# Output weights' scale through GpSimd ahead of the scores, two conversions moved into slots, and 40 idle products on PE before block 0's value product

## The chip, the cores and the metric

One core of a Trainium2 chip runs the kernel. The metric is device time in microseconds (us) of one launch. A profiled execution gives, beside its own time, a trace of each engine: PE (TensorE, matrix products; PEld is its weight load), DVE (VectorE), ACT (ScalarE), POOL (GpSimd) and SP (SyncE, which here only issues DMAs).

## What is computed

An attention layer and two feed-forward layers, in float32, on 12,288 tokens of width 128:

```python
kv_pool = kv.reshape(B, H // 4, 4, W // 4, 4, C).mean(axis=(2, 4))   # 768 keys
k = v = kv_pool.reshape(B, -1, C) @ w_sr
a = softmax(q @ k.T / sqrt(C));  x = a @ v
h = x @ moe_w_in;   g = h * clip(h + 3, 0, 6) / 6;   x = g @ moe_w_out    # 128 -> 2048 -> 128
h = x @ moe2_w_in;  g = where(h >= 1, h, where(h <= -1, 0, (h + 1)**2 / 4))
out = g @ moe2_w_out
```

## The kernel before

**Split numbers.** Each factor of the large products is cut into a high and a low part (fp16 in attention's value product and layer 0, fp32r elsewhere) and three products are summed. Weights are cut on the chip. For layer 0 they are scaled first by a power of two and a unit taken from the largest magnitude of the whole matrix; this needs a maximum over all 128 partitions. `mw[1]` collects it for layer 0's output weights, `w_sc[1]` holds the scales (`ws` in the rows).

**Weight conversion.** A piece is 128 x 512 numbers, 16 pieces j0 to j15: of layer 0 the pieces j0, j2, j4, j6 are input weights, j1, j3, j5, j7 output weights. A conversion has four stages: j.0 two ACT passes (L237, L241 or L244), j.1 two DVE passes (L251, L253) and a GpSimd add (L255), j.2 one DVE pass (L261), j.3 the high part on ACT (L272) and the low part on GpSimd (L275; for j5 on DVE).

**Order.** `tc.manual_schedule()` keeps on each engine the order in which the code records instructions, so an engine that waits holds everything behind it. Waits between engines come from the tiles: whoever reads or writes a tile waits for its earlier writer or readers, and a tile counts as a whole. The work has two phases.

*Prologue* (about 0 to 64 us): the string `PROLOGUE` names steps one by one: pooling of kv, keys, block 0's scores (s, S), maxima (n, N), exponentials (e), the normalised weights' high and low part (a, b; b also issues the DMA transpose into `at`), the scale of v (vm, vr, vs), its high part on ACT (vh, L405) and low part on DVE (vl, L410) out of the PSUM tiles `vps` (`acc` in the rows), the value product (x0, x1, L533) and the first conversions. Steps m1, m3, m5, m7 are the four DVE maxima over the output weights (L178), oa their row maximum (L184). ot and ob find the maximum over the partitions with a PE transpose, a DVE reduction and a PE product with `ones` (L193, L197, L198), oc makes the scales (L205 to L214), hs the layer's factors `h_sc` and `o_sc`. For the input weights the same maximum goes through GpSimd (ia: L184, L187).

*Slots.* Slot T handles a 256-wide piece of layer 0's hidden width, and from T = 11 also one of layer 1: `m_in` (L554) on PE, `relu1` on ACT (L597), `mul1` on DVE (L603), the split `hi_lo` on ACT and GpSimd (L631, L633), `m_out` (L570) on PE; a block of 512 tokens takes 8 slots. A slot also carries steps of the next blocks' scores (L461, L472, L497), normalisation (L505 to L518) and value product. `conv_step` starts a conversion in each slot listed in `CONV_AT` and moves each one in flight on by a stage.

Of the kernel before, what the change touches and what calls it, by code (L numbers as in the profile page):

```python
# [8 lines left out]
FP32 = mybir.dt.float32  # L9
# [6 lines left out]
ALU = mybir.AluOpType  # L16
AX = mybir.AxisListType
# [8 lines left out]
KV_MODE = "DDVVPPPPPPPP"  # L26
PROLOGUE = """
m0 k0 k1 m2 m4 m6 ia k2 ib g2 k4 k3 j0.0 g3 t1 j2.0 j0.1 k5 p1 q0 k6 z1 t2 j0.2 j2.1 p2 t0 j0.3 k7 p0
z0 j2.2 j4.0 k8 t3 z2 j2.3 k9 j4.1 p3 s0 y3 k10 z3 j4.2 j6.0 y2 k11 n0 t4 j4.3 y1 s2 t5 j6.1 p4
p5 n2 z4 z5 y5 s1 j6.2 y4 n1 y0 S2 S0 N0 m1 S1 N1 j6.3 s3 n3 N2 e0 e1 vm S3 a0 vr b0 e2 a1 m3  # L30
N3 e3 a2 b1 vs a3 vh b2 b3 vl m5 m7 oa ot q1 ob oc hs j1.0 x0 j1.1 j3.0 x1 j1.2 j3.1 j1.3 j3.2 j5.0 j3.3
j5.1
"""
N_ST = 6
W_DT = (FP16, F32R)

H_SC = 2.0 ** -22
# [13 lines left out]
def tile_attn_moe_moe2(  # L51
# [15 lines left out]
    nc = tc.nc  # L67
# [20 lines left out]
    sm_p = ctx.enter_context(tc.tile_pool(name="sm", bufs=3))  # L88
# [29 lines left out]
    def new_h():  # L118
        return ps_h.tile([128, 512], FP32, tag="h", name="h")
# [50 lines left out]


    mw = [const.tile([128, 4], FP32, name=f"mw{n}") for n in range(4)]
    w_tops = {}

    def w_max(job):
        m, which, i = job
# [2 lines left out]
                                axis=AX.X, op=ALU.max, apply_absolute_value=True)  # L179

    def w_top(n):
        nc.vector.tensor_reduce(out=mw[n][:, 0:1], in_=mw[n], axis=AX.X, op=ALU.max)  # L184

    def w_top_pool(n):
        nc.gpsimd.partition_all_reduce(mw[n][:, 1:2], mw[n][:, 0:1], channels=128,  # L187
                                       reduce_op=bass_isa.ReduceOp.max)
        w_tops[n] = mw[n][:, 1:2]

    def w_top_row(n):
        w_tops[n] = new_h()
        nc.tensor.transpose(w_tops[n][0:1, 0:128], mw[n][:, 0:1], ident)  # L193

    def w_top_all(n):
        m1 = sm_p.tile([1, 1], FP32, tag="wtop", name="wtop")
        nc.vector.tensor_reduce(out=m1, in_=w_tops[n][0:1, 0:128], axis=AX.X, op=ALU.max)  # L197
        nc.tensor.matmul(w_tops[n][:, 128:129], ones, m1)  # L198
        w_tops[n] = w_tops[n][:, 128:129]

    def w_scales(n):
        sc, u, v = w_sc[n], w_sc[n].bitcast(U32), mw[n].bitcast(U32)
        nc.vector.tensor_scalar(out=mw[n][:, 0:1], in0=w_tops[n], scalar1=2.0 ** -14, scalar2=None,  # L205
                                op0=ALU.max)
# [524 lines left out]
    with tc.manual_schedule():  # L731
        nc.scalar.dma_start(out=wsr, in_=w_sr)
        load_next()
        make_identity(nc, ident)
        nc.vector.memset(ones, 1.0)
        nc.vector.tensor_reduce(
            out=pool_m.rearrange("p (a q) -> p a q", a=4),
            in_=ident.rearrange("p (a r q) -> p a q r", a=4, r=4), axis=AX.X, op=ALU.add,
        )
        nc.vector.tensor_scalar(out=pool_m, in0=pool_m, scalar1=1.0 / 16.0, scalar2=None, op0=ALU.mult)  # L740
        mem = {}

# [76 lines left out]
```

## Time and profile before

| | |
|---|---|
| three timed runs | 1333.38, 1334.45, 1334.20 us, median 1334.2 |
| profiled execution | 1333.9 us, of it 1332.1 us span (first to last instruction) |
| busy in the span | PE 1279.0, DVE 1145.1, ACT 1049.2, POOL 1017.3 us |
| granted PE clock, mean | 0.987 of 2.4 GHz |

The page's busy times are means over unlike stages. A stretch of the trace is read by itself: which engine is busy in it throughout, and, where none is, which instruction ends each wait.

### The profile page before, as it was taken

The page shows a single profiled execution, that of the slowest core. Times are in us where ns is not written, and L with a number is a line of the kernel's source. Part 1 is how long each engine was busy: PE and PEld are TensorE (multiplying, and loading weights), DVE is VectorE, ACT ScalarE, POOL GpSimd, SP SyncE. Part 2 cuts the span into 40 slices and gives each one's busy share as a digit, 9 for nine tenths or more (in the row PEclk, how much of TensorE's full clock was granted, in tenths as well). Part 3 has the DMA queues.
Part 4 walks back from the last instruction along what each step waited for, and adds up shares of the span by engine and source line. Part 5 has one row for each costly group of instructions (what it writes and reads, how often), then busy time and mean ns, then how long its engine had stood idle before and what let it go on. Part 6 is the DMA issues. An engine that isn't in the chain of part 4 may idle for free.

```text
span 1332.1 us, 18501 instructions
## 1 busy us (share of the span) xinstructions
PE 1279.0 (96%) x6250; PEld 843.8 (63%) x6250; DVE 1145.1 (86%) x1851; ACT 1049.2 (79%) x1917; POOL 1017.3 (76%) x826
## 2 busy tenths in 40 slices
PE   6578899999999999999999999999999999999998
PEld 5434566666666666666666666666666666666666
DVE  4789998898888888989989889888888899898677
ACT  2588988887788788788878778887887888788776
POOL 1278897787787787877878877877877778787886
PEclk9789999999999999999999999999999999999999
DMA  9633122222221212212123122222312121121001
GB/s 327 149 78 66 28 43 45 40 44 44 41 44 32 52 33 44 48 29 51 36 40 52 33 44 40 45 39 45 42 35 52 32 45 36 32 45 24 8 9 16
DMA packets 260783, 66.28 MB, mean 50 GB/s; under 512 B 252368, under 2 KB 256592, under 8 KB 260688
## 3 DMA queue, kind: packets, MB, share of 16 engines
q1 hardware_dynamic: 257888, 63.73, 24.9%
q10 hardware_dynamic: 2800, 1.38, 0.4%
q8 instruction: 49, 0.80, 0.3%
q14 instruction: 46, 0.38, 0.1%
HBM read 21.04 MB, written 6.29 MB: 21 GB/s over the span
## 4 chain that ended last, share of the span: by engine, by line
PE 82%; DVE 5%; ACT 2%; issue 1%; POOL 0%; POOLq 0%; ACTq 0%; DVEq 0%
PE acc L570 35%; PE h L554 35%; PE s L461 6%; PE s L533 6%; DVE g L610 1%; DVE g L620 1%; DVE t L603 1%; ACT t L597 1%; ACT h L631 1%; DVE a L518 1%; POOL l L633 0%; DVE wa L251 0%; DVE nm L472 0%; ACT g L616 0%; DVE wst L261 0%
## 5 line engine op out<-in xcount | busy, mean ns | idle before, releaser
L633 POOL TENSOR_TENSOR l<-g,h 128x512 fp32r<-128x512 f32 x382 | 503.0, 1337 | 238.8 <-ACT h L631 111.7
L633 POOL TENSOR_TENSOR l<-t,h 128x512 f16<-128x512 f32 x382 | 445.2, 1187 | 11.4 <-ACT h L631 11.4
L597 ACT ACTIVATE t<-h,h_sc 128x512 f32<-128x512 f32 x384 | 244.4, 687 | 172.1 <-PE h L554 168.1
L603 DVE SCALAR_TENSOR_TENSOR t<-t,h 128x512 f32<-128x512 f32 x384 | 245.9, 681 | 112.5 <-ACT t L597 112.2
L620 DVE TENSOR_TENSOR g<-h,g 128x512 f32<-128x512 f32 x384 | 245.8, 681 | 14.1 <-ACT g L616 7.5
L631 ACT CAST h<-t 128x512 f16<-128x512 f32 x384 | 224.9, 619 | 36.0 <-DVE t L603 35.1
L610 DVE TENSOR_SCALAR g<-h 128x512 f32<-128x512 f32 x384 | 246.1, 682 | 1.1 <-POOL l L633 0.7
L616 ACT ACTIVATE g<-g 128x512 f32<-128x512 f32 x384 | 227.8, 628 | 1.1 <-DVE g L610 0.9
L631 ACT CAST h<-g 128x512 fp32r<-128x512 f32 x384 | 217.2, 616 | 6.5 <-PE acc L570 3.7
L554 PE MATMUL h<-x2h,wi1h 128*128 128x512 f32 x384 | 183.7, 478 | 3.5 <-DVE g L620 3.0
L570 PE MATMUL acc<-h,wo1h 128*128 128x512 f32 x384 | 185.0, 482 | 0.7 <-DVE o L588 0.6
L554 PE MATMUL h<-xh,wi0h 128*128 128x512 f16 x384 | 148.0, 385 | 4.7 <-DVE t L603 2.3
L570 PE MATMUL acc<-l,wo1h 128*128 128x512 f32 x384 | 151.4, 395 | 0.7 <-POOL l L633 0.7
L554 PE MATMUL h<-x2l,wi1h 128*128 128x512 f32 x384 | 151.8, 395 | 0.0
L554 PE MATMUL h<-x2h,wi1l 128*128 128x512 f32 x384 | 151.6, 395 | 0.0
L570 PE MATMUL acc<-h,wo1l 128*128 128x512 f32 x384 | 151.6, 395 | 0.0
L570 PE MATMUL acc<-l,wo0h 128*128 128x512 f16 x384 | 146.5, 382 | 3.2 <-POOL l L633 3.1
L570 PE MATMUL acc<-h,wo0h 128*128 128x512 f16 x384 | 148.4, 386 | 0.4 <-DVE su L505 0.4
L570 PE MATMUL acc<-h,wo0l 128*128 128x512 f16 x384 | 146.1, 380 | 0.0
L554 PE MATMUL h<-xl,wi0h 128*128 128x512 f16 x384 | 146.0, 380 | 0.1
L554 PE MATMUL h<-xh,wi0l 128*128 128x512 f16 x384 | 146.0, 380 | 0.0
L554 PEld LDWEIGHTS <-wi0h 128*128 128x128 f16 x768 | 61.0, 98 | 102.6 <-issue 55.1
(170 smaller groups left out, 1960.9 us busy)
## 6 DMA issues: line engine op xcount, KB each, us to landing
out_dram<-o SPq DMA_DIRECT2D x96, 64.0 KB, 2.0
q<-in_q_dram SPq DMA_DIRECT2D x92, 64.0 KB, 2.5
wst<-in_kv_dram SPq DMA_DIRECT2D x6, 512.0 KB, 7.0
wst<-in_moe_w_out_dram SPq DMA_DIRECT2D x6, 512.0 KB, 9.1
wst<-in_moe_w_in_dram SPq DMA_DIRECT2D x3, 512.0 KB, 6.3
at<-a SPq DMA_TRANSPOSE x96, 3.7
g<-in_moe_w_in_dram SPq DMA_DIRECT2D x2, 512.0 KB, 4.7
h<-in_kv_dram SPq DMA_DIRECT2D x2, 512.0 KB, 8.3
```

What stands on the lines that cost most here:

```text
L461: nc.tensor.matmul(ps[h], l[:, js], r[:, ks], start=(n == 0), stop=(n == 2))
L518: nc.vector.scalar_tensor_tensor(out=a[:, 1], in0=e, scalar=rc, in1=a[:, 0], op0=ALU.mult, op1=ALU.subtract)
L533: nc.tensor.matmul(ps, l[:, k, :], r[:, k, :], start=(n == 0), stop=(n == 3 * KC - 1))
L554: nc.tensor.matmul(ps, l[:, ws], r, start=(n == 0), stop=(n == 2))
L570: nc.tensor.matmul(acc[m], l[:, ws], r[:, k, :], start=(c == 0 and i == 0), stop=(c == NPAIR - 1 and i == 5))
L597: nc.scalar.activation(out=g_t[0, s][:, k], in_=h_t[0, s, k], func=ACTF.Relu, scale=h_sc, bias=0.5 * H_SC)
L603: nc.vector.scalar_tensor_tensor(out=g, in0=g, scalar=H_SC, in1=h_t.pop((0, s, k)), op0=ALU.min, op1=ALU.mult)
L610: nc.vector.tensor_scalar(out=g_t[1, s][:, k], in0=h_t[1, s, k], scalar1=1.0, scalar2=-1.0, op0=ALU.min, op1=ALU.max)
L616: nc.scalar.activation(out=g, in_=g, func=ACTF.Square, scale=0.5, bias=0.5)
L620: nc.vector.tensor_tensor(out=g, in0=h_t.pop((1, s, k)), in1=g, op=ALU.max)
L631: nc.scalar.copy(out=hi[:, k], in_=g[:, k])
L633: eng.tensor_tensor(out=lo[:, k], in0=g[:, k], in1=h, op=ALU.subtract)
```

## The change

Six edits, all in the prologue's order and in `CONV_AT`:

- the four maxima and their row maximum (m1, m3, m5, m7, oa) stand ahead of the second halves of block 0's scores, and the maximum over partitions goes through GpSimd's `partition_all_reduce`, as for the input weights; ot and ob are gone;
- the scales (oc) stand behind the first normalisation (a0), so DVE waits there for GpSimd's result;
- j6 and j5 leave the prologue, and j3 keeps only two of its four stages there; `CONV_AT` has 11 slots in place of 9;
- j1 starts behind oc, ahead of the value product;
- q1 (transposed and split q of block 1) stands behind x1;
- `wu`, 40 products of `ident` with `ident` into columns 384 to 511 of `vps[0]`, whose result nobody uses, stands ahead of vl.

```diff
-z0 j2.2 j4.0 k8 t3 z2 j2.3 k9 j4.1 p3 s0 y3 k10 z3 j4.2 j6.0 y2 k11 n0 t4 j4.3 y1 s2 t5 j6.1 p4
-p5 n2 z4 z5 y5 s1 j6.2 y4 n1 y0 S2 S0 N0 m1 S1 N1 j6.3 s3 n3 N2 e0 e1 vm S3 a0 vr b0 e2 a1 m3
-N3 e3 a2 b1 vs a3 vh b2 b3 vl m5 m7 oa ot q1 ob oc hs j1.0 x0 j1.1 j3.0 x1 j1.2 j3.1 j1.3 j3.2 j5.0 j3.3
-j5.1
+z0 j2.2 j4.0 k8 t3 z2 j2.3 k9 j4.1 p3 s0 y3 k10 z3 j4.2 y2 k11 n0 t4 j4.3 y1 s2 t5 p4
+p5 n2 z4 z5 y5 s1 m1 m3 y4 n1 y0 S2 S0 N0 m5 m7 oa S1 N1 s3 n3 N2 e0 e1 vm S3 a0 oc vr b0 j1.0 e2 a1
+N3 e3 a2 j1.1 b1 vs a3 vh b2 b3 wu vl x0 j1.2 j3.0 hs x1 j1.3 q1 j3.1
-CONV_AT = (1, 2, 4, 6, 7, 8, 10, 12, 14)
+CONV_AT = (0, 2, 4, 5, 6, 7, 8, 9, 10, 12, 14)
     def w_top(n):
         nc.vector.tensor_reduce(out=mw[n][:, 0:1], in_=mw[n], axis=AX.X, op=ALU.max)
-    def w_top_pool(n):
         nc.gpsimd.partition_all_reduce(mw[n][:, 1:2], mw[n][:, 0:1], channels=128,
                                        reduce_op=bass_isa.ReduceOp.max)
-    def w_top_row(n):
-        w_tops[n] = new_h()
-        nc.tensor.transpose(w_tops[n][0:1, 0:128], mw[n][:, 0:1], ident)
-    def w_top_all(n):
-        m1 = sm_p.tile([1, 1], FP32, tag="wtop", name="wtop")
-        nc.vector.tensor_reduce(out=m1, in_=w_tops[n][0:1, 0:128], axis=AX.X, op=ALU.max)
-        nc.tensor.matmul(w_tops[n][:, 128:129], ones, m1)
+        def warm():
+            for _ in range(40):
+                nc.tensor.matmul(vps[0][:, 384:512], ident, ident)
+        steps["wu"] = warm
```

Line numbers of the changed kernel are 16 lower than those of before in most of the file (L405 becomes L389). On PE, between the last product of v's scale and the first product of x0 (`h<-at,vh`), before and then changed; `acc_127` is `vps[0]`, and in brackets stands whose signal an instruction waits for:

```order
L377 MATMUL acc_128<-m_470,ones 128x1 [waits DVE_49]
L193 MATMUL h<-ident,mw_121 1x128 [waits DVE_49]
L198 MATMUL h<-wtop,ones 128x1 [waits DVE_49]
L533 LDWEIGHTS vh [waits DMAHW7_49]
L533 MATMUL h<-at,vh 128x256 [waits DMAHW6_49]
```

```order
L361 MATMUL acc_128<-m_471,ones 128x1 [waits DVE_49]
L772 MATMUL acc_127<-ident 128x128 [waits Activation_49]
L772 MATMUL acc_127<-ident 128x128 x39
L517 LDWEIGHTS vh [waits DMAHW7_49]
L517 MATMUL h<-at,vh 128x256 [waits DMAHW6_49]
L517 LDWEIGHTS vh
L517 MATMUL h<-at,vh 128x256
L517 LDWEIGHTS vl [waits DVE_49]
```

The two small products are gone, the 40 idle ones stand there; the first of them waits for ACT's first half of vh, which reads the same tile, and x0's third product waits for DVE's vl. On DVE, the low part of v before, and the same in the changed kernel, with what follows:

```order
L410 SCALAR_TENSOR_TENSOR vl<-acc_127,sv,vh 128x384 [waits Activation_49]
L410 SCALAR_TENSOR_TENSOR vl<-acc_128,sv,vh 128x384 [waits Activation_49]
L178 TENSOR_REDUCE mw_121<-wst 128x1 [waits DMAHW7_49]
L178 TENSOR_REDUCE mw_121<-wst 128x1 [waits DMAHW0_49]
L184 TENSOR_REDUCE mw_121<-mw_121 128x1 [waits DVE_49]
```

```order
L394 SCALAR_TENSOR_TENSOR vl<-acc_127,sv,vh 128x384 [waits PE_49,Activation_49]
L394 SCALAR_TENSOR_TENSOR vl<-acc_128,sv,vh 128x384 [waits Activation_49]
L523 SCALAR_TENSOR_TENSOR xl<-h,xh 128x256 [waits Activation_49]
L245 SCALAR_TENSOR_TENSOR t_226<-t_226,wa 128x512 [waits DMAHW4_49,Pool_49]
L203 TENSOR_SCALAR mw_121<-mw_121 128x1
```

vl now waits for PE as well: for the last of the 40 products, which are recorded ahead of it and write its source tile. On POOL, in the changed kernel, the second reduction over partitions and its neighbours (the rows named ISA load code: L182 that of the reduction, L239 the usual one again):

```order
L259 TENSOR_TENSOR wi0l<-l_146,wi0h 128x512 [waits DMAHW7_49,Activation_49]
L182 ISA
L182 ISA mw_121<-mw_121 128x1 [waits DVE_49]
L239 ISA
L239 TENSOR_TENSOR wa<-wa,wr 128x512 [waits DVE_49,Activation_49,Pool_49]
```

Before, no code load stands here: the add L255 of j6 follows L275.

## Rows read from the trace of the kernel before

**Rows 1.** Stretches: busy time of each engine, granted PE clock, DMA share.

```profile
core 0: us, PE busy (x) PEld busy (x) DVE busy (x) ACT busy (x) POOL busy (x), PEclk, DMA share, GB/s
50.00:60.00 10.00, 2.32 (x10) 1.61 (x11) 8.50 (x26) 4.30 (x7) 1.26 (x1) 0.50 0.92 166
90.00:100.00 10.00, 8.59 (x42) 5.20 (x43) 9.90 (x14) 7.77 (x15) 8.03 (x6) 0.83 0.32 58
300.00:500.00 200.00, 200.00 (x981) 131.94 (x980) 177.08 (x283) 159.65 (x294) 155.74 (x128) 1.00 0.23 41
```

**Rows 2.** Timeline (start, length, engine, line): block 0 to slot 0's ReLU.

```profile
47.43 1.00 DVE L518 SCALAR_TENSOR_TENSOR a<-e,rc,a 128x768 f16<-128x768 f32 x1
53.53 1.03 ACT L405 ACTIVATE vh<-acc,sv 128x384 f16<-128x384 f32 x2
54.60 1.13 DVE L410 SCALAR_TENSOR_TENSOR vl<-acc,sv,vh 128x384 f16<-128x384 f32 x2
...
58.57 0.61 PE L533 MATMUL h<-at,vh 128*128 128x256 f16 x2
...
64.43 0.38 PE L554 MATMUL h<-xh,wi0h 128*128 128x512 f16 x1 [0.47 <-ACT xh L538]
...
70.31 1.25 ACT L597 ACTIVATE t<-h,h_sc 128x512 f32<-128x512 f32 x2
```

**Rows 3.** Timeline of POOL: the one reduction over partitions, and the prologue's third split.

```profile
13.89 0.38 POOL L187 PARTITION_ALL_REDUCE mw<-mw  x1 [12.38 <-DVE mw L184]
25.68 1.25 POOL L255 TENSOR_TENSOR wa<-wa,wr 128x512 int32<-128x512 int32 x1 [11.41 <-ACT e L347]
...
37.26 1.45 POOL L275 TENSOR_TENSOR wi0l<-l,wi0h 128x512 f16<-128x512 f32 x1 [1.50 <-ACT wi0h L272]
```

**Rows 4.** Line L255 up to 27 us: its instructions on POOL's queue.

```profile
L255 POOLq MODIFY_POOL_CONFIG  x2: 83/83/83, 14.2 to 14.3; - x2
L255 POOLq EVENT_SEMAPHORE  x1: 17/17/17, 20.0 to 20.0; - x1
```

**Rows 5.** Timeline of DVE: scales, the two passes of stage .1, a maximum.

```profile
16.24 0.15 DVE L205 TENSOR_SCALAR mw<-mw 128x1 f32<-128x1 f32 x1
...
17.06 0.16 DVE L214 TENSOR_TENSOR ws<-ws,w_k 128x3 f32<-128x3 f32 x1
...
19.11 0.42 DVE L251 TENSOR_SCALAR wa<-wa 128x512 f32<-128x512 f32 x1
19.56 0.43 DVE L253 TENSOR_SCALAR wa<-wa 128x512 uint32<-128x512 uint32 x1
...
37.72 1.27 DVE L253 TENSOR_SCALAR wa<-wa 128x512 uint32<-128x512 uint32 x1
...
42.97 0.67 DVE L178 TENSOR_REDUCE mw<-t 128x1 f32<-128x512 f32 x1
```

**Rows 6.** Timeline of PE's weight loads: two float32 products, 128 x 128 each.

```profile
31.34 0.30 PEld L352 LDWEIGHTS h<-e,wsr 128*128 128x128 f32 x2 [0.20 <-ACT e L347]
...
31.56 0.30 PEld L353 LDWEIGHTS acc<-wsr,e 128*128 128x128 f32 x2
```

**Rows 7.** Stretches of 1 us around two rises of the granted clock.

```profile
60.00:61.00 1.00, 1.00 (x7) 0.71 (x5) 0.84 (x7) 0.86 (x2) 0.00 (x0) 0.50 0.74 117
61.00:62.00 1.00, 1.00 (x10) 0.84 (x9) 0.00 (x0) 0.63 (x1) 0.00 (x0) 0.88 0.11 17
...
74.00:75.00 1.00, 0.74 (x2) 0.75 (x3) 0.94 (x4) 1.00 (x4) 1.00 (x1) 0.50 0.81 288
78.00:79.00 1.00, 1.00 (x5) 0.45 (x4) 0.73 (x1) 1.00 (x3) 1.00 (x1) 0.85 0.00 0
```

**Rows 8.** Timeline of ACT: the last conversion pass ahead of slot 0's ReLU.

```profile
69.75 0.65 ACT L272 CAST wo0h<-wst 128x512 f16<-128x512 f32 x1 [1.83 <-DVE wst L261]
```

**Rows 9.** Timeline of DVE in the slots, beside a busy POOL.

```profile
103.75 1.26 DVE L253 TENSOR_SCALAR wa<-wa 128x512 uint32<-128x512 uint32 x1
...
107.42 1.63 DVE L261 SCALAR_TENSOR_TENSOR g<-g,wa 128x512 uint32<-128x512 uint32 x1 [0.35 <-POOL wa L255]
```

More of the change, by code (lines that the diff above doesn't have):

```diff
@@ L172, in tile_attn_moe_moe2 @@
     mw = [const.tile([128, 4], FP32, name=f"mw{n}") for n in range(4)]
-    w_tops = {}
     def w_max(job):
@@ L184, in w_top @@
         nc.vector.tensor_reduce(out=mw[n][:, 0:1], in_=mw[n], axis=AX.X, op=ALU.max)
-    def w_top_pool(n):
         nc.gpsimd.partition_all_reduce(mw[n][:, 1:2], mw[n][:, 0:1], channels=128,
                                        reduce_op=bass_isa.ReduceOp.max)
-        w_tops[n] = mw[n][:, 1:2]
-    def w_top_row(n):
-        w_tops[n] = new_h()
-        nc.tensor.transpose(w_tops[n][0:1, 0:128], mw[n][:, 0:1], ident)
-    def w_top_all(n):
-        m1 = sm_p.tile([1, 1], FP32, tag="wtop", name="wtop")
-        nc.vector.tensor_reduce(out=m1, in_=w_tops[n][0:1, 0:128], axis=AX.X, op=ALU.max)
-        nc.tensor.matmul(w_tops[n][:, 128:129], ones, m1)
-        w_tops[n] = w_tops[n][:, 128:129]
     def w_scales(n):
         sc, u, v = w_sc[n], w_sc[n].bitcast(U32), mw[n].bitcast(U32)
-        nc.vector.tensor_scalar(out=mw[n][:, 0:1], in0=w_tops[n], scalar1=2.0 ** -14, scalar2=None,
+        nc.vector.tensor_scalar(out=mw[n][:, 0:1], in0=mw[n][:, 1:2], scalar1=2.0 ** -14, scalar2=None,
                                 op0=ALU.max)
@@ L767, in tile_attn_moe_moe2 @@
             steps[f"m{n}"] = lambda n=n: w_max(w_jobs[n])
-        steps |= {"ia": lambda: (w_top(0), w_top_pool(0)), "ib": lambda: (w_scales(0), w_unit(0)),
-                  "oa": lambda: w_top(1), "ot": lambda: w_top_row(1), "ob": lambda: w_top_all(1),
-                  "oc": lambda: w_scales(1)}
+        for n, k in enumerate("io"):
+            steps[k + "a"] = lambda n=n: w_top(n)
+            steps[k + "b"] = lambda n=n: (w_scales(n), w_unit(n))
+            steps[k + "c"] = lambda n=n: w_scales(n)
         for j in range(4):
```

## The prediction

> **What bounds the kernel now.** I read the stretches first. From 300 to 500 us PE is busy for all 200 us at full clock and DVE for 177 [rows 1]: PE sets the pace there, the change touches nothing there, and whatever shifts the start of this steady part shifts the end by as much. The change acts in the first 140 us, where PE is not the bound: from 50 to 60 us it works 2.3 of 10 us at a granted clock of 0.50 (1.2 of 2.4 GHz), and from 90 to 100, in the slots, DVE is busy 9.9 of 10 [rows 1]. So I follow one chain through the timeline, engine by engine: the first low part of block 0's attention weights at 47.43 (DVE), v's high part at 53.53 (ACT), x0's first product at 58.57 (PE), slot 0's first product at 64.43 and its ReLU at 70.31 (ACT) [rows 2]. The reader is to see in these rows five links; the change alters each, and behind the last one there is DVE's work in the slots. The sum is made against the profiled execution, 1333.9 us (1332.1 span), 0.3 under the median of the runs.
>
> **A. To the first low part: +3.4 (bounds -0.9 and +4.3).** DVE loses j6 here: 0.42 + 1.27 for its two passes [rows 5], and about 0.7 for the third. It gains three of the four maxima at 0.67 [rows 5], which stood further back. So DVE and, with it, ACT come to the low part 0.9 us earlier, near 46.5, if nothing else holds them. But oc, six small DVE instructions of 1.0 us in all (16.24 to 17.22 for their like [rows 5]), now stands ahead of it and waits for GpSimd. The only reduction in the trace has a price that its 0.38 us don't show: the next GpSimd instruction starts at 25.68, 11.8 us after the reduction's 13.89 [rows 3], though its last operand was signalled at 20.0 and the load of the usual code was put into the queue at 14.2 [rows 4]. In the changed kernel the load of the reduction's code comes behind the split that ends at 38.71 [rows 3]. In one reading a load runs from its place in the queue: load and reduction together take 11.8, the result is there at 50.5, and the low part starts 1.0 + 0.3 later at 51.8: +4.3. In another the load starts only when its first user is ready; what is proven late at 25.68 is 5.7 us; with the row maximum done near 42.7 the result comes at 48.8 at the earliest and the low part at 50.1: +2.6. If a load takes 5.7 from its place, it is over at 44.4 and nothing is held: -0.9. The first reduction speaks against the second reading: it came with 12.4 us of idle time before it and started as soon as its operand was there [rows 3]. Between a whole 11.8 and something shorter no row decides. The nearest row is the one load seen from its place to its user, 11.4 us, so I stay near it and take the middle of the first two, +3.4.
>
> The Trainium skill (GPSIMD Engine Reference, section 2.1, Instruction dispatch) says that the first call of freshly loaded GpSimd code pays about 6 us more, which no profile instruction shows. The 5.7 us past the signal at 20.0 [rows 4] agree; the first reduction [rows 3] doesn't, it shows no delay. By that rule alone A would be about +2.9 and the sum 0.5 smaller.
>
> **B. From there to v's high part: +0.2.** j1's two passes, 0.42 + 0.43, come in, one maximum of 0.67 goes out [rows 5]. Bounds 0 and +1.
>
> **C. From v's high part to x0: +6.1 (bounds +4.4 and +13.2).** Before, this takes 58.57 - 53.53 = 5.0 [rows 2], since PE had the two small products of ob to do. Now the 40 products start when ACT's first half of vh is done, 0.5 us after its start (1.03 for two [rows 2]): they write the tile that vh reads. x0 is queued behind them, and so is vl on DVE, which reads the same tile and waits for the last of them. A float32 product of 128 x 128 is two PE instructions, and two products' loads start 0.22 us apart [rows 6], so 0.11 an instruction and 8.8 us for 80 at full clock; at half clock 17.6. The engine has idled before, as before 58.57, so it begins at 0.50. There it reaches the full level at about 61.1, 2.5 us after 58.57, and later at about 78.3, some 4 us after it set in near 74.3 [rows 7]. I take 3.5 us at half clock (16 instructions) and 64 x 0.11 = 7.0 at full: 10.5. So 0.5 + 0.1 + 10.5 - 5.0 = +6.1. Nothing hides it: ACT, DVE and POOL have no instruction left that doesn't wait for x0 but j1's add. The transposed weights arrive earlier than the products end, so their arrival doesn't count any more.
>
> **D. From x0 to slot 0's first product: -0.9.** Before, 5.86 us [rows 2], with 58.57 to 61.1 at half clock [rows 7]; at full clock this part is half as long, -1.25. Against it x0's third product waits for vl's first half, which starts only behind the idle products: 0.57 (half of 1.13 [rows 2]) less the two products ahead, +0.35. Bounds -1.3 and 0.
>
> **E. To slot 0's ReLU: -4.1.** Before, 5.9 us [rows 2]: two passes of j5 and the casts of j1 and j3, the last at 69.75 after a wait of 1.83 [rows 8], stand ahead of the ReLU on ACT. Now only j1's cast (0.55 between starts) and the cast of q, which waits for DVE's transpose, stand there: some 1.8. Bounds -4.6 and -3. What is late next is block 1's scores: they need q's low part from GpSimd, queued behind j1's split.
>
> **F. The conversions moved into the slots: +3.5 (bounds +1.5 and +6).** After the ReLU two more pairs of stage .1 and one more stage .2 are to be done on DVE than before: 2 x 0.85 + 0.7 = 2.4 beside an idle POOL [rows 5], about 5 at slot durations (1.26 for one pass, 1.63 for stage .2 [rows 9]). DVE is the busiest engine there [rows 1], though with some waits that can take up work. I take the middle. From slot 10 on both kernels start the same conversions, so nothing is gained back.
>
> **Sum.** 3.4 + 0.2 + 6.1 - 0.9 - 4.1 + 3.5 = +8.2: 1342.1 us on the profiled execution, and 1342 as the time. The weight loads on SP keep their order up to the fourth transpose; later ones come earlier or later by a slot and are needed from slot 10, so I cost them at nothing (late, they would hold slot 10's conversion).
>
> **Rivals.**
> *1. GpSimd costs only what its records say (not slower).* If the code is there by 44.4, that is, if a load takes 5.7 us or less from its place in the queue, A is -0.9, and if DVE's passes in the slots keep their undisturbed 0.42 and 0.43, F is 2.4: -0.9 + 0.2 + 6.1 - 0.9 - 4.1 + 2.4 = +2.8, 1336.7, within 0.2%; with C at its bound of +4.4, 1335. For it: the first reduction was not delayed. Against it: 25.68.
> *2. The idle products never reach full clock.* C is +13.2, the sum +15.3: 1349. For it: granted clocks of 0.50 beside busy PE [rows 7]. Against it: both rises there came with PE busy.
> *3. The clock pays in the slots.* Before, PE's products of slots 0 and 1 run at half clock from about 74 to 78.3 [rows 7]. If the idle products keep it at full clock and the slots hang on PE after all, half of these 4 us comes back and DVE's extra work hides beside it (F near 0): 1342.1 - 2.1 - 3.5 = 1336.5. Against it: DVE at 9.9 of 10 [rows 1].
> *4. The idle products warm nothing*, that is, the chain waits for the transposes anyway and C is 0. Against it: x0 is queued behind them by order, and even at full clock they take 8.8 us from 0.5 us after vh starts.
>
> **How the numbers follow.** Forecast 0.58, rival 1 0.20, rival 2 0.07, rival 3 0.12, rival 4 0.03. This kernel's runs tell about 0.2% from no change, so faster is below 1331.5 and slower above 1336.9. The forecast's own range is 1337 to 1347; it and rival 2 are slower (0.65). Rivals 1 and 3 scatter around the upper edge of no change: of their 0.32 I give 0.09 to slower, 0.15 to the same and 0.08 to faster, where A and F both reach their lower ends; rival 4 (1336, with E and D) adds 0.01 to each. Faster 0.09, same 0.16, slower 0.75. The range reaches down into rivals 1 and 3, to 1333.5, and up to 1348, where A and C are both near their upper ends.
>
> **What would show it.** GpSimd's second reduction, and DVE's first instruction of the scales right behind it, start between 48 and 51 with DVE idle for 4 us or more before (A). PE's idle products run from about 58 to 68.5, the first third of that at 0.50; vl starts when they end, not with vh (C). Slot 0's ReLU starts near 75, under 2.5 us after slot 0's first product (E), and slot 11's some 8 us later than before. The forecast is wrong if DVE passes the scales without a wait by 46, if the products take under 7 us, or if slot 11 has made up what slot 0 lost.

## The result, and the profile after

The changed kernel takes 1354.2 us (median of four runs, 1353.6 to 1355.2) against 1334.3 for the kernel before beside it: ratio 1.015, 95% interval 1.0132 to 1.0168. It is slower, as forecast, but by 19.9 us instead of 8, and so outside the range of 1333.5 to 1348. The profiled execution takes 1353.6, of it 1351.5 span.

Of the busy times over the whole span only PE's has grown by much: 1291.5 us against 1279.0, most of it the 11.5 of the idle products; DVE has 1147.3, ACT 1049.1, POOL 1016.3, all within 2.2 of before. So the loss is work that stands at a worse place, and waiting. The stretches of the changed kernel show where:

```profile
50.00:60.00 10.00, 3.65 (x17) 3.65 (x18) 5.98 (x17) 5.17 (x10) 1.25 (x1) 0.50 0.76 138
60.00:70.00 10.00, 9.44 (x80) 9.01 (x80) 1.14 (x2) 0.00 (x0) 0.00 (x0) 0.94 0.11 20
70.00:80.00 10.00, 7.49 (x45) 4.49 (x42) 8.61 (x18) 7.21 (x13) 5.99 (x5) 1.00 0.18 28
90.00:100.00 10.00, 7.10 (x26) 3.98 (x27) 8.52 (x11) 8.81 (x16) 7.16 (x5) 0.83 0.50 107
...
110.00:120.00 10.00, 8.20 (x36) 4.69 (x37) 6.59 (x10) 5.68 (x10) 6.54 (x7) 0.71 0.22 42
120.00:130.00 10.00, 4.41 (x18) 1.71 (x16) 6.13 (x7) 5.18 (x10) 6.54 (x5) 0.80 0.36 79
...
300.00:500.00 200.00, 200.00 (x973) 131.79 (x972) 178.06 (x284) 161.38 (x296) 157.26 (x130) 1.00 0.24 42
```

The last row is that of [rows 1] again: the steady part is untouched. From 60 to 70 little but PE works, most of the time on the idle products. New are the rows from 110 to 130: no engine is busy for more than 8.2 of 10 us, DVE, by the prediction the busiest engine of the slots, for 6.6 and 6.1. Something there waits in a circle. The five links of [rows 2] in the changed kernel, in its timeline (start, length, engine, line; in brackets the idle time before and what ended it):

```profile
48.05 1.00 DVE L502 SCALAR_TENSOR_TENSOR a<-e,rc,a 128x768 f16<-128x768 f32 x1
...
55.73 1.03 ACT L389 ACTIVATE vh<-acc,sv 128x384 f16<-128x384 f32 x2
...
56.35 11.50 PE L772 MATMUL acc<-ident 128*128 128x128 f32 x80 [7.59 <-ACT vh L389]
67.69 0.38 PE L517 MATMUL h<-at,vh 128*128 128x256 f16 x2
...
67.96 1.14 DVE L394 SCALAR_TENSOR_TENSOR vl<-acc,sv,vh 128x384 f16<-128x384 f32 x2 [11.08 <-PE acc L772]
...
72.99 0.38 PE L538 MATMUL h<-xh,wi0h 128*128 128x512 f16 x1 [0.47 <-ACT xh L522]
...
74.57 1.26 ACT L581 ACTIVATE t<-h,h_sc 128x512 f32<-128x512 f32 x2
```

So the low part comes 0.6 later, vh 2.2, x0 9.1, slot 0's first product 8.6, and its ReLU 4.3 later than before. This part went nearly as forecast (4.7). From there the two kernels drift apart:

| start of the first ReLU of slot | 0 | 5 | 6 | 7 | 8 | 13 | 19 |
|---|---|---|---|---|---|---|---|
| before | 70.31 | 99.28 | 103.10 | 109.15 | 114.13 | 146.40 | 186.66 |
| changed | 74.57 | 106.03 | 113.55 | 120.04 | 130.30 | 165.75 | 206.02 |
| difference | 4.3 | 6.8 | 10.5 | 10.9 | 16.2 | 19.4 | 19.4 |

The two largest steps, into slot 6 and into slot 8, are waits of PE for weights of layer 0 (timelines of ACT, POOL and PE; L256 makes a piece's high part, L259 its low part, L538 is `m_in`, L554 `m_out`):

```profile
109.30 0.66 ACT L256 CAST wi0h<-l 128x512 f16<-128x512 f32 x1
...
110.01 0.61 PE L538 MATMUL h<-xh,wi0h 128*128 128x512 f16 x1 [3.11 <-ACT wi0h L256]
...
111.46 1.32 POOL L259 TENSOR_TENSOR wi0l<-l,wi0h 128x512 f16<-128x512 f32 x1
...
112.84 0.61 PE L538 MATMUL h<-xh,wi0l 128*128 128x512 f16 x1 [1.79 <-POOL wi0l L259]
...
123.31 0.65 ACT L256 CAST wo0h<-wst 128x512 f16<-128x512 f32 x1
...
124.02 0.39 PE L554 MATMUL acc<-h,wo0h 128*128 128x512 f16 x1 [3.11 <-ACT wo0h L256]
...
125.71 1.33 POOL L259 TENSOR_TENSOR wo0l<-wst,wo0h 128x512 f16<-128x512 f32 x1
...
127.09 0.61 PE L554 MATMUL acc<-h,wo0l 128*128 128x512 f16 x1 [2.47 <-POOL wo0l L259]
```

Each product starts right when the weight that it multiplies by is finished. `CONV_AT` starts j6 in slot 2 and j7 in slot 4, a conversion does a stage a slot, so j6 ends at the end of slot 5 and j7 at the end of slot 7. The last two pairs of a block, slots 6 and 7, need j6 (`m_in` of slot 6) and j7 (`m_out` of slot 6, recorded in slot 7 right behind the stage that makes the weight). These four waits are 3.1 + 1.8 + 3.1 + 2.5 = 10.5 us. While PE waits, ACT, DVE and GpSimd wait for PE's products: that is the circle.

### The profile page after: what moved, and what is told of

Read it like the earlier page. It is cut to its first block, busy times and chain, and to the rows that moved or that the text cites. A ratio compares the mean times of both kernels' runs of the same rounds, so it can differ in the third digit from the quotient of the medians.

```text
span 1351.5 us, 18661 instructions
## 1 busy us (share of the span) xinstructions
PE 1291.5 (96%) x6327; PEld 853.5 (63%) x6327; DVE 1147.3 (85%) x1850; ACT 1049.1 (78%) x1917; POOL 1016.3 (75%) x827
## 4 chain that ended last, share of the span: by engine, by line
PE 83%; DVE 4%; ACT 2%; POOL 0%; issue 0%; POOLq 0%; DVEq 0%; ACTq 0%
PE acc L554 35%; PE h L538 35%; PE s L445 6%; PE s L517 6%; DVE g L594 1%; DVE t L587 1%; DVE g L604 1%; DVE a L502 0%; POOL l L617 0%; ACT t L581 0%; DVE wa L235 0%; ACT h L615 0%; DVE wst L245 0%; DVE nm L456 0%; DVE wa L237 0%
## 5 line engine op out<-in xcount | busy, mean ns | idle before, releaser
L538 PE MATMUL h<-x2h,wi1h 128*128 128x512 f32 x384 | 184.0, 479 | 2.8 <-DVE g L604 2.2
L554 PE MATMUL acc<-h,wo1h 128*128 128x512 f32 x384 | 185.1, 482 | 1.0 <-DVE o L572 0.6
L538 PE MATMUL h<-xh,wi0h 128*128 128x512 f16 x384 | 148.8, 387 | 7.2 <-DVE t L587 3.7
L538 PE MATMUL h<-x2l,wi1h 128*128 128x512 f32 x384 | 152.1, 396 | 0.0
L554 PE MATMUL acc<-l,wo1h 128*128 128x512 f32 x384 | 151.4, 395 | 0.7 <-POOL l L617 0.7
L538 PE MATMUL h<-x2h,wi1l 128*128 128x512 f32 x384 | 151.9, 396 | 0.0
L554 PE MATMUL acc<-h,wo1l 128*128 128x512 f32 x384 | 151.6, 395 | 0.0
L554 PE MATMUL acc<-h,wo0h 128*128 128x512 f16 x384 | 147.9, 385 | 3.7 <-ACT wo0h L256 3.1
L554 PE MATMUL acc<-l,wo0h 128*128 128x512 f16 x384 | 146.3, 381 | 2.7 <-POOL l L617 2.6
L538 PE MATMUL h<-xh,wi0l 128*128 128x512 f16 x384 | 147.0, 383 | 1.8 <-POOL wi0l L259 1.8
L554 PE MATMUL acc<-h,wo0l 128*128 128x512 f16 x384 | 146.3, 381 | 2.5 <-POOL wo0l L259 2.5
L538 PE MATMUL h<-xl,wi0h 128*128 128x512 f16 x384 | 146.9, 383 | 0.1
L538 PEld LDWEIGHTS <-wi0h 128*128 128x128 f16 x768 | 61.2, 99 | 105.7 <-issue 55.3
```

The source lines that it names most:

```text
L538: nc.tensor.matmul(ps, l[:, ws], r, start=(n == 0), stop=(n == 2))
L554: nc.tensor.matmul(acc[m], l[:, ws], r[:, k, :], start=(c == 0 and i == 0), stop=(c == NPAIR - 1 and i == 5))
```

## The experiments

All slot times below are from one profiled execution each. The input loads bound the first 36 us, and the last PE product that hangs on them (the transpose of the pooled kv) starts between 35.6 and 37.4 us in these profiles, so a slot 0 compares to about 1 us only. How far it is from slot 0 to slot 13 does not follow that (82.5 to 82.6 in e2, e3, e5 and e6, whose inputs differ by 1.4 us), and is the column to read. Each ratio is to runs of before beside it; small differences between groups of runs are read from ratios, not from medians.

| | median | ratio to before, 95% | slot 0 | slot 13 | 0 to 13 |
|---|---|---|---|---|---|
| before | 1334.3 to 1334.8 | | 70.31 | 146.40 | 76.1 |
| changed | 1354.2 | 1.0132 to 1.0168 | 74.57 | 165.75 | 91.2 |
| e1 no products | 1346.2 | 1.0073 to 1.0122 | 67.07 | 157.98 | 90.9 |
| e2 j6, j7 earlier | 1346.3 | 1.0074 to 1.0104 | 75.19 | 157.76 | 82.6 |
| e3 both | 1338.0 | 1.0017 to 1.0041 | 66.47 | 149.04 | 82.6 |
| e4 maximum on PE | 1352.4 | 1.0114 to 1.0148 | 73.29 | 164.17 | 90.9 |
| e5 products in own tile | 1337.2 | 1.0015 to 1.0035 | 66.70 | 149.28 | 82.6 |
| e6 e3 + maximum on PE | 1336.2 | 1.0006 to 1.0025 | 66.30 | 148.84 | 82.5 |
| e7 conversions moved alone | 1336.1 | 1.0003 to 1.0029 | 68.47 | 149.17 | 80.7 |
| e8 wait filled | 1328.9 | 0.9947 to 0.9977 | 61.98 | 140.75 | 78.8 |
| e9 e7, other list | 1339.1 | 1.0019 to 1.0042 | 68.19 | 151.39 | 83.2 |
| e10 e8 with GpSimd | 1331.8 | 0.9968 to 0.9987 | 65.48 | 144.33 | 78.9 |
| e11 e9, three buffers | 1337.0 | 1.0006 to 1.0028 | 68.05 | 149.20 | 81.2 |
| e12 e8, three buffers | 1330.4 | 0.9949 to 0.9978 | 63.62 | 142.16 | 78.5 |

**e1: no products.**

```diff
-N3 e3 a2 j1.1 b1 vs a3 vh b2 b3 wu vl x0 j1.2 j3.0 hs x1 j1.3 q1 j3.1
+N3 e3 a2 j1.1 b1 vs a3 vh b2 b3 vl x0 j1.2 j3.0 hs x1 j1.3 q1 j3.1
```

> The changed kernel without the 40 idle products. My theory: they cost what stands between vh and x0, and nothing gives it back. Without them x0 waits only for the transposed weights, its first product comes 4 to 6 us after vh starts instead of 11.96, slot 0's ReLU near 68 instead of 74.57, and since layer 0's late conversions are paced by slots, the rest of the loss stays: 1347 (1346 to 1349) against 1354.2. Rival: the products pay back in the slots by the full clock that they leave; then x0 is as early, but PE's products of slots 0 and 1 run at half clock and the time is 1350 or more.

Measured 1346.2: the products cost 8.0 us. x0 starts 2.7 after vh instead of 11.96, released by the transposes' DMA; that was earlier than the 4 to 6 expected. Slot 0 comes 7.5 us earlier, and the way from slot 0 to 13 stays at 90.9, as the theory had it. The rival's condition, half clock in slots 0 and 1 without the products, did not come about: the granted clock is 1.00 from 66 to 80 us in this run too. So this run does not price a lower clock there.

**e2: j6 and j7 started earlier.**

```diff
-CONV_AT = (0, 2, 4, 5, 6, 7, 8, 9, 10, 12, 14)
+CONV_AT = (0, 1, 2, 5, 6, 7, 8, 9, 10, 12, 14)
```

> The changed kernel with j6 started in slot 1 and j7 in slot 2 (they start in slots 2 and 4), j8 and later as they are; all that is computed is the same. My theory: slots 6 and 7 of the changed kernel wait for weights whose last stage stands one slot or no slot ahead of their first product (PE idle 3.1 + 1.8 us for wi0, 3.1 + 2.5 us for wo0). With one and two slots more these four waits go, slot 8's ReLU comes 8 to 10 us earlier than 130.30, and the time is 1345 (1344 to 1347). Rival: DVE's total work of conversions is the bound in the slots, and the waits are only where it shows; then slot 6 is earlier, later slots lose it again and the time is 1350 to 1354.

Measured 1346.3, 7.9 less than the changed kernel and within the range; slot 8's ReLU comes 6.9 us earlier (123.45 against 130.30), less than the 8 to 10 expected. Timelines of ACT and PE in this run, around slots 6 and 7:

```profile
109.59 0.39 PE L538 MATMUL h<-xh,wi0l 128*128 128x512 f16 x1 [0.55 <-POOL wi0l L259]
...
111.01 0.64 ACT L256 CAST wo0h<-wst 128x512 f16<-128x512 f32 x1
```

j7's high part is ready 12 us earlier than at 123.31, and of the four waits 0.55 us is left. The way from slot 0 to 13 shrinks by 8.6, from 91.2 to 82.6, and later slots do not lose it again: the rival, DVE's work as the bound behind these waits, falls.

**e3: both edits.**

```diff
-N3 e3 a2 j1.1 b1 vs a3 vh b2 b3 wu vl x0 j1.2 j3.0 hs x1 j1.3 q1 j3.1
+N3 e3 a2 j1.1 b1 vs a3 vh b2 b3 vl x0 j1.2 j3.0 hs x1 j1.3 q1 j3.1
-CONV_AT = (0, 2, 4, 5, 6, 7, 8, 9, 10, 12, 14)
+CONV_AT = (0, 1, 2, 5, 6, 7, 8, 9, 10, 12, 14)
```

> Both edits together: no idle products, and j6 and j7 started in slots 1 and 2. My theory, with two costs that add up: 1338 (1336 to 1341), that is, still some 4 us above the kernel before, which is the added work of conversions in the slots. Rival: they overlap (an earlier start of the slots meets conversions and scores that are no earlier): 1343 or more.

Measured 1338.0: 8.0 + 7.9 are 15.9 of the 19.9, and together they give 16.2. The costs add. What the trace shows in front of x0 (timeline of PE):

```profile
58.75 0.58 PE L517 MATMUL h<-at,vh 128*128 128x256 f16 x2 [9.62 <-DMA at<-a]
```

PE has been idle for 9.6 us there, and what ends this is the DMA transpose. DVE idles 4.4 us at the same place, from 58.5 to 62.9.

**e4: the maximum on PE, as before, at the early place.**

```diff
-p5 n2 z4 z5 y5 s1 m1 m3 y4 n1 y0 S2 S0 N0 m5 m7 oa S1 N1 s3 n3 N2 e0 e1 vm S3 a0 oc vr b0 j1.0 e2 a1
+p5 n2 z4 z5 y5 s1 m1 m3 y4 n1 y0 S2 S0 N0 m5 m7 oa S1 ot N1 s3 n3 N2 e0 e1 ob vm S3 a0 oc vr b0 j1.0 e2 a1
```

> The changed kernel with the maximum over partitions found on PE and DVE as before (transpose, row maximum, product with ones), at the early place; GpSimd's second reduction and its code loads are gone. My theory: DVE's wait of 3.3 us ahead of the scales goes and half of the next one, block 0's first low part starts near 46 instead of 48.05, vh 2 us earlier, and all behind it: 1352 (1351 to 1353). Rival: GpSimd's code loads are the larger part of the loss (its reload holds j1's add until 53.9 and what follows): 1347 or less.

Measured 1352.4, as expected. DVE's wait ahead of the scales does not go, it shrinks (timeline of DVE):

```profile
46.27 0.16 DVE L204 TENSOR_SCALAR mw<-h 128x1 f32<-128x1 f32 x1 [1.24 <-PE h L197]
```

1.2 us for PE's product instead of 3.29 for GpSimd. The low part starts at 47.39, not near 46; but the inputs ended 1.5 later in this execution (37.27 against 35.74), and from there to vh it is 17.8 us against 20.0. (1352.4 and 1354.2 have intervals that overlap; the runs themselves do not.)

**e5: products in a tile of their own.** On top of e2's list, at the same place in the text, and 30 of them in place of 40:

```diff
-            for _ in range(40):
-                nc.tensor.matmul(vps[0][:, 384:512], ident, ident)
+            w = new_h()
+            for _ in range(30):
+                nc.tensor.matmul(w[:, :128], ident, ident)
```

> As the run with both edits (j6 and j7 in slots 1 and 2), but with 30 idle products in a PSUM tile of their own, so that they wait for nothing and nothing but PE's order waits for them; they fit into PE's idle 49 to 58.7 us. My theory: the price of the products in the changed kernel is the shared tile (they wait for vh, vl and x0 wait for them), not the work. So x0 starts at 58.7 as without products, now at full clock, slot 0's ReLU comes 0.5 to 1 us earlier than the 66.47 without products, and since DVE bounds the first slots nearly nothing of it is left: 1337.5 (1336.8 to 1338.2). Rival 1: products cost their own time wherever they stand: 1341 or more. Rival 2: a warm PE is worth more in the slots: 1336 or less.

Measured 1337.2. Timeline of PE:

```profile
49.36 8.33 PE L773 MATMUL h<-ident 128*128 128x128 f32 x60
59.20 0.38 PE L517 MATMUL h<-at,vh 128*128 128x256 f16 x2 [1.51 <-DMA at<-a]
```

The products run in the idle time, x0 waits for the same transposes as without them and starts at full clock (0.38 us where e3 shows 0.58). Yet the second half of x waits for its transposes again and slot 0 is not earlier: 66.70 against 66.47. So the price in the changed kernel is the shared tile, and the full clock during x0 is worth nothing measurable (0.8 in the medians, whose runs spread by as much). 40 products in a tile of their own were not run; the 30 end 1.5 us before the transposes are there.

**e6: e3 with the maximum on PE.** The steps of e4 on top of e3:

```diff
-p5 n2 z4 z5 y5 s1 m1 m3 y4 n1 y0 S2 S0 N0 m5 m7 oa S1 N1 s3 n3 N2 e0 e1 vm S3 a0 oc vr b0 j1.0 e2 a1
+p5 n2 z4 z5 y5 s1 m1 m3 y4 n1 y0 S2 S0 N0 m5 m7 oa S1 ot N1 s3 n3 N2 e0 e1 ob vm S3 a0 oc vr b0 j1.0 e2 a1
```

> No idle products, j6 and j7 in slots 1 and 2, and the maximum over partitions on PE and DVE instead of GpSimd. Three costs taken away that each was measured alone (8.0, 7.9, 1.9). My theory: they add: 1336.2 (1335.5 to 1337). Rival: without products x0 waits for the DMA transposes, so that DVE's earlier low parts are worth less: 1337.5 or more.

Measured 1336.2, the number of the theory. The trace is nearer to the rival: slot 13 is only 0.2 earlier than in e3. With inputs 1.3 later than in e3's profile the two can't be told apart, and I leave it open whether the three costs add fully.

**e7: the moved conversions alone, on the kernel before.** j6.0 to j6.3, j5.0 and j5.1 are struck from `PROLOGUE`, and:

```diff
-CONV_AT = (1, 2, 4, 6, 7, 8, 10, 12, 14)
+CONV_AT = (0, 1, 2, 5, 6, 7, 8, 9, 10, 12, 14)
```

> The kernel before with one edit: j6 and j5 leave the prologue, and the slots start 0: j5, 1: j6, 2: j7, then 5, 6, 7, 8, 9, 10, 12, 14. My theory: the prologue gets shorter by 2 to 3.5 us at slot 0's ReLU (70.31 before), DVE then has the two conversions in slots where it has no gap left, and by slot 13 (146.40) the kernel is 2 to 4 us later than before: 1337 (1336 to 1338.5). Rival: conversions in slots fit into waits that DVE has there anyway; then slot 13 keeps the gain of the prologue: 1332 or less.

Measured 1336.1. Slot 0 gains 1.8, and the way to slot 13 grows by 4.6. Stretches of this run:

```profile
80.00:100.00 20.00, 15.62 (x74) 8.24 (x74) 19.79 (x29) 15.58 (x27) 14.79 (x11) 0.91 0.50 99
100.00:120.00 20.00, 16.27 (x83) 9.25 (x81) 16.77 (x24) 17.54 (x32) 15.81 (x13) 0.91 0.39 83
120.00:140.00 20.00, 13.70 (x59) 6.42 (x56) 19.61 (x26) 16.82 (x30) 17.14 (x13) 0.91 0.19 34
```

DVE (third pair) is busy 19.8 and 19.6 of 20 us in the first and the last of them, where before it was 18.2 and 18.1; only between them it idles, for 3.2. Over the whole way from slot 0 to 13 it is busy 4.7 us more than before, and the way is 4.6 longer: its waits did not take up the two conversions.

**e9: another list.**

```diff
-CONV_AT = (0, 1, 2, 5, 6, 7, 8, 9, 10, 12, 14)
+CONV_AT = (0, 1, 2, 3, 4, 6, 7, 8, 10, 12, 14)
```

> The kernel before with j6 and j5 out of the prologue, as in the run with that edit alone, but the conversions in the slots spread otherwise: 0, 1, 2, 3, 4, 6, 7, 8, 10, 12, 14 instead of 0, 1, 2, 5, 6, 7, 8, 9, 10, 12, 14. With the other list slot 9's ReLU was at 120.89 and slot 13's at 149.17, 2.5 us more in these four slots than before. My theory: that part is bunching (conversions started in six slots in a row, 5 to 10, while DVE had 3 us idle from 100 to 120), so it goes: slot 13 near 146.5 to 147.5, 1334 (1333 to 1335.3). Rival: DVE's work is the same in sum and has to be done by slot 13: 1336 as with the other list.

Measured 1339.1: both theories fall. Slots 9 to 13 take 25.7 us as before, so the loss there is gone, but slots 3 to 7 lose more than it. Timelines of DVE and ACT:

```profile
92.78 0.68 DVE L260 SCALAR_TENSOR_TENSOR l<-l,wa 128x512 uint32<-128x512 uint32 x1
...
93.49 0.68 ACT L236 ACTIVATE wa<-g 128x512 f32<-128x512 f32 x1 [2.30 <-DVE l L260]
...
94.63 1.24 ACT L596 ACTIVATE t<-h,h_sc 128x512 f32<-128x512 f32 x2
```

The pool of work buffers has two of `wa`. A conversion that starts in the third slot in a row needs the buffer that DVE's stage .2 of the first one frees, DVE is late, and slot 4's ReLU stands behind the waiting pass on ACT.

**e11: e9 with three work buffers** of `wa` and of `wr`.

```diff
-    wk_p = ctx.enter_context(tc.tile_pool(name="wk", bufs=2))
+    wk_p = ctx.enter_context(tc.tile_pool(name="wk", bufs=3))
```

> The run with conversions started in slots 0, 1, 2, 3, 4, 6, 7, 8, 10, 12, 14, with three work buffers (wa, wr) instead of two. In that run (1339.0, slot 4's ReLU at 94.63, slot 13's at 151.39) a conversion started in a third slot in a row waits on ACT for DVE's stage .2 of the one two slots before, which frees its buffer: 2.30 us ahead of slot 4's ReLU, 1.68 ahead of slot 5's, and the ReLU is queued behind. My theory: these waits are what a dense list costs; with a third buffer they go, slot 4 comes near 91.5 to 92.5, slot 13 at 147 to 149, 1336 (1334.5 to 1337). Rival: DVE's work in slots 0 to 7 is the bound and ACT only waits where DVE is late anyway; then slot 13 stays within 1 us of 151.39: 1338 or more.

Measured 1337.0, 2.1 less than e9 (1.9 by the ratios, 1.0031 and 1.0017, whose intervals overlap). Timeline of ACT, then a stretch:

```profile
90.74 0.67 ACT L236 ACTIVATE wa<-g 128x512 f32<-128x512 f32 x1
...
91.86 1.24 ACT L596 ACTIVATE t<-h,h_sc 128x512 f32<-128x512 f32 x2
```

```profile
86.00:102.00 16.00, 10.88 (x51) 5.49 (x50) 15.70 (x25) 13.59 (x24) 11.29 (x9) 0.89 0.57 107
```

The wait is gone and slot 4 comes at 91.86. Then DVE is busy for 15.7 of 16 us, and slot 13 ends at 149.20, where e7 with its other list has 149.17. So the part of the theory on the buffers holds. That the rest of the loss is the rival's, DVE's sum of work, is argued only: two unlike lists end at the same place, but e7's list was not run with three buffers.

**e8: the wait for the transposes filled**, no products, the maximum on PE:

```diff
-p5 n2 z4 z5 y5 s1 m1 m3 y4 n1 y0 S2 S0 N0 m5 m7 oa S1 N1 s3 n3 N2 e0 e1 vm S3 a0 oc vr b0 j1.0 e2 a1
-N3 e3 a2 j1.1 b1 vs a3 vh b2 b3 wu vl x0 j1.2 j3.0 hs x1 j1.3 q1 j3.1
+p5 n2 z4 z5 y5 s1 m1 m3 y4 n1 y0 S2 S0 N0 m5 m7 oa S1 ot N1 s3 n3 N2 e0 e1 ob vm S3 a0 oc vr b0 e2 j1.0 a1
+N3 e3 a2 j1.1 b1 vs a3 vh b2 b3 j3.0 vl q1 j1.2 hs j3.1 j1.3 x0 j5.0 j3.2 x1 j5.1 j3.3
-CONV_AT = (0, 2, 4, 5, 6, 7, 8, 9, 10, 12, 14)
+CONV_AT = (0, 1, 2, 4, 6, 7, 8, 10, 12, 14)
```

> A version to beat both: no idle products, the early maxima with the maximum over partitions on PE, and the conversions j1, j3 (whole) and j5's first two stages put into the stretch in which DVE, ACT and GpSimd wait for block 0's transposed weights, with q of block 1 there too; j6 starts in slot 0, j7 in 1, j8 in 2, then 4, 6, 7, 8, 10, 12, 14. My theory: DVE's idle 4.4 us ahead of x0 take 2.5 to 4 us of work that cost its full length in the slots: slot 13 at about the 146.4 of before or 1 to 2 earlier, 1333 (1331.5 to 1334.5). Rival: more conversion work beside the scores only moves the wait to ACT ahead of slot 0's ReLU: 1335 or more.

Measured 1328.9, ratio to before 0.9962 (0.9947 to 0.9977): it beats both kernels, by more than expected. Timelines of PE and DVE:

```profile
54.56 0.65 DVE L260 SCALAR_TENSOR_TENSOR t<-t,wa 128x512 uint32<-128x512 uint32 x1
...
54.61 0.58 PE L532 MATMUL h<-at,vh 128*128 128x256 f16 x2 [8.06 <-DMA at<-a]
...
57.00 0.42 DVE L250 TENSOR_SCALAR wa<-wa 128x512 f32<-128x512 f32 x1
```

Between vl and the first half of x DVE now does q of block 1, j1's stage .2, the layer's factors and j3's stage .1, at their short durations; x0 waits for the transposes anyway. Slot 0 comes 4.3 earlier than in e6, and the way to slot 13 is 3.8 shorter. Of the 4.3, 1.6 is from earlier inputs. Another 1.6 has nothing to do with the filled wait: j1.0 now stands behind e2, DVE's wait of 1.61 us for e2 (e6, at 50.02) is gone, and from the inputs to vh it is 16.2 us against 17.8.

**e10: e8 with GpSimd's reduction**, as in the changed kernel (ot and ob are gone again):

```diff
-p5 n2 z4 z5 y5 s1 m1 m3 y4 n1 y0 S2 S0 N0 m5 m7 oa S1 ot N1 s3 n3 N2 e0 e1 ob vm S3 a0 oc vr b0 e2 j1.0 a1
+p5 n2 z4 z5 y5 s1 m1 m3 y4 n1 y0 S2 S0 N0 m5 m7 oa S1 N1 s3 n3 N2 e0 e1 vm S3 a0 oc vr b0 e2 j1.0 a1
```

> The version that fills the wait for the transposes, with GpSimd's reduction in place of the product path on PE. My theory: the reduction's result comes 8.5 us after the split before it and so some 2 us after the 44.73 at which the scales start with the product path, and the reload of the usual code keeps j1's add until about 53.9, 4.7 later than its 49.23, where DVE now waits for it: 1.5 to 3 us in sum, 1331 (1330 to 1332.5). Rival: both hide, since x0 waits for DMA transposes: 1329.5 or less.

Measured 1331.8. Timelines of POOL and DVE:

```profile
47.09 0.38 POOL L182 PARTITION_ALL_REDUCE mw<-mw  x1 [8.31 <-issue]
...
47.51 0.15 DVE L189 TENSOR_SCALAR mw<-mw 128x1 f32<-128x1 f32 x1 [2.82 <-POOL mw L182]
...
54.90 1.97 POOL L239 TENSOR_TENSOR wa<-wa,wr 128x512 int32<-128x512 int32 x1 [7.43 <-ACT a L495]
```

The scales start 2.8 us later than the 44.73 of e8, of which 1.5 is from later inputs, and the add 5.7 later than 49.23, which delays DVE's stage .2 from 54.56 to 57.33. It is 2.9 us in the medians and 2.1 by the ratios (0.9978 and 0.9962, whose intervals overlap), both within what was expected.

**e12: e8 with three work buffers**, the same edit as in e11.

```diff
-    wk_p = ctx.enter_context(tc.tile_pool(name="wk", bufs=2))
+    wk_p = ctx.enter_context(tc.tile_pool(name="wk", bufs=3))
```

> The best version so far (1328.9) with three work buffers. Its waits of ACT for a work buffer are 1.2 us in sum in the slots. My theory: at most that is to be had: 1328.3 (1327.5 to 1329.2). Rival: DVE is the bound there and nothing changes, or ACT's passes earlier disturb the scores: 1329 or more.

Measured 1330.4, by the ratio (0.9964 against 0.9962) the same as e8: nothing gained. Slot 0 is 1.6 later in its profile, ahead of any slot, and the way to slot 13 0.3 shorter; why slot 0 is later was not followed up.

## Why the prediction failed

**A, to the first low part: +3.4 forecast, +0.6 measured.** The mechanism was right, its size wrong. DVE did wait for GpSimd, 3.29 us, and the scales started at 46.94 instead of "between 48 and 51". The load's place came 0.7 earlier than in the sum (38.0 and not 38.71), and load and reduction took 8.9 from it and not 11.8. Timelines of DVE and POOL, then POOL's queue for the two code loads:

```profile
41.52 0.16 DVE L181 TENSOR_REDUCE mw<-mw 128x1 f32<-128x4 f32 x1
...
46.53 0.38 POOL L182 PARTITION_ALL_REDUCE mw<-mw  x1 [8.78 <-issue]
53.87 1.25 POOL L239 TENSOR_TENSOR wa<-wa,wr 128x512 int32<-128x512 int32 x1 [6.96 <-ACT a L495]
```

```profile
L182 POOLq MODIFY_POOL_CONFIG  x2: 11/11/11, 37.9 to 38.0; - x2
...
L239 POOLq MODIFY_POOL_CONFIG  x2: 82/82/83, 46.9 to 46.9; - x2
L239 POOLq EVENT_SEMAPHORE  x1: 43/43/43, 53.0 to 53.0; - x1
```

The load of the reduction's code is put into the queue at 38.0 and its user starts 8.5 us later, 4.9 after its operand (41.68). Alone, this fits a load that runs from its place in the queue as well as one that starts with its user. The load of the usual code behind it tells them apart: its user starts 7.0 us after the place (46.9) and 0.9 after the operand (53.0); in e10, where the operand comes earlier against the load, 7.4 after the place and 3.0 after the operand. The time from the place stays, the other does not: that is the first reading, with 8.5 in place of 11.8. Why the load of before took 11.4 from its place [rows 3, rows 4] no run shows. The Trainium skill (GPSIMD Engine Reference, section 2.1, Instruction dispatch) has about 6 us paid by the first call; here 4.9, 0.9 and 3.0 were paid behind the operand, and 7.0 to 8.5 from the place on, so the one figure fits none of them.

**B, to vh: +0.2 forecast, +1.6 measured.** I counted DVE's instructions only. j1's two passes stand on ACT ahead of e2 and start when the scales are there (48.02), and DVE then waits 1.61 us for e2. In e8, where j1 starts behind e2, this wait is gone. Timeline of DVE:

```profile
50.66 0.16 DVE L479 TENSOR_TENSOR su<-s 128x1 f32<-128x1 f32 x1 [1.61 <-ACT e L475]
```

**C, to x0: +6.1 forecast, +6.9 measured.** The products took 11.50 us instead of 10.5: they ran at half clock until about 61.2 (0.50 up to 60, 0.94 from 60 to 70), 4.8 us and not 3.5. And the comparison with before hid a part of their price: without them x0 would have started 2.7 us after vh (e1) and not 5.0, because the two products of ob are gone. The early maxima had made room, and the idle products took it.

**D and E: -0.9 and -4.1 forecast, -0.6 and -4.3 measured.** To slot 0's ReLU the sum is +4.3 against +4.7. That is luck: A came out 2.8 too high, B and C together 2.2 too low.

**F, "the conversions moved into the slots: +3.5 (bounds +1.5 and +6)": +15.1 measured. This step failed.** It counted what DVE has to do, 2.4 to 5 us, and took the middle. The runs split the 15.1, the growth from slot 0 to slot 13 (91.2 against 76.1). Stretches from slot 0's to slot 13's first ReLU in before, e7, e3 and the changed kernel:

```profile
70.31:146.40 76.09, 58.59 (x263) 33.52 (x264) 68.59 (x97) 64.02 (x115) 60.65 (x45) 0.89 0.34 70
68.47:149.17 80.70, 60.48 (x269) 33.06 (x270) 73.29 (x103) 67.96 (x119) 61.83 (x46) 0.89 0.33 66
66.47:149.04 82.57, 62.90 (x282) 35.58 (x281) 76.89 (x106) 68.53 (x121) 65.20 (x49) 0.90 0.34 67
74.57:165.75 91.18, 65.33 (x282) 35.83 (x282) 77.70 (x106) 68.61 (x120) 64.25 (x49) 0.87 0.30 61
```

- 8.6 (e2) are PE's waits for j6 and j7, for which the step had no term. It never asked when a moved conversion is due. "Needed from slot 10" and "from slot 10 on both kernels start the same conversions" held for what is loaded late, not for the two pieces of layer 0 in slots 6 and 7, though the list, a stage a slot and eight slots a block gave the due slots by counting.
- 4.6 (e7) are DVE's work for j5 and j6: DVE (third pair) is busy 73.3 us where before it was 68.6, and idles 7.4 where before it was 7.5.
- 1.9 (e3 against e7) are DVE's work for j3, which the step left out. It counted two more pairs of stage .1 and one more stage .2; the changed kernel has three and two. j3's stage .1 begins 0.6 us ahead of slot 0's ReLU, its stage .2 behind it: three instructions and 3.6 us of DVE more than in e7. That q1, recorded ahead of it, put it there is argued only.

So the step's own term measured 6.5 and not 3.5, above its upper bound. The "waits that can take up work" took up 1.8: in e3 DVE has 8.3 us more to do than before on a way 6.5 longer.

**The rivals.** Rival 1 was nearer in A (-0.9 against +0.6 measured), but the code was not there by its 44.4, and its F of 2.4 is farther off. Rival 2 is out: the granted clock is 0.94 from 60 to 70. Rival 3 is out by the changed kernel itself: its clock is 1.00 from 70 to 80 us, where before it was 0.50 from 74 [rows 7], and yet the way from slot 0 to slot 2 takes 10.6 us (74.57 to 85.20) against 10.1 before (70.31 to 80.42). Rival 4 is half true, in that x0 waits for the transposes without them; but until 2.7 us after vh, not 12.

## What to carry to other kernels

When work is moved to a later place, write down for each moved piece the instruction that first needs it, and count the stages between; then count every stage that crosses the border, also those of pieces that move only in part. Here the first was worth 8.6 us and the second 6.5. An idle filler on PE cost nothing in a tile that nobody else reads or writes (e5); in a shared one it was a barrier on both sides, for 8.0 us (e1). And before filler is put into a wait, look for work that costs its full length elsewhere: the same wait for the transposes gave some 5 to 6 us when it took up conversions, with the list of slots that goes with that (7.2 between e6 and e8, less the 1.6 of j1's later start), and nothing when it took up idle products (e5).

## What the chip showed besides

In the profiles of e1 and e3 the way from slot 19 to 24 takes 37.3 and 36.2 us, in all others 31.1 to 31.3. It is one instruction. Timelines of DVE and POOL in e1, and the same place in e2:

```profile
201.38 5.51 DVE L502 SCALAR_TENSOR_TENSOR a<-e,rc,a 128x768 f16<-128x768 f32 x1
...
201.33 2.53 POOL L617 TENSOR_TENSOR l<-g,h 128x512 fp32r<-128x512 f32 x2
203.82 2.26 POOL L617 TENSOR_TENSOR l<-t,h 128x512 f16<-128x512 f32 x2
```

```profile
201.20 2.05 DVE L502 SCALAR_TENSOR_TENSOR a<-e,rc,a 128x768 f16<-128x768 f32 x1
...
201.13 3.26 POOL L617 TENSOR_TENSOR l<-g,h 128x512 fp32r<-128x512 f32 x2
```

Alone this pass takes 1.0 us [rows 2]. In e2 the two engines slow each other; in e1 DVE's pass starts 0.05 us behind a row of four GpSimd instructions and ends 0.8 us after the last of them. The Trainium skill (SBUF — State Buffer, SBUF: two separate sides) says that DVE with two SBUF inputs and a reading GpSimd instruction share a port pair that one of them holds for a whole instruction; the trace agrees, and shows that the loser can lose four times in a row. A single profile of this kernel can so be 4 to 6 us off its median, and e1 and e3 were: 1352.3 against 1346.2, and 1341.8 against 1338.0.
